# Where the first constants, logarithms and chunk-end powers are issued in a gated-attention and feed-forward kernel

## The chip, the cores and the metric

The kernel runs on one core of a Trainium2 chip. A core has a matrix engine (TensorE, PE in the profile), three engines for elementwise work (VectorE or DVE, ScalarE or ACT, GpSimd or POOL), and a fifth, SyncE or SP, that only issues DMA transfers. ScalarE and GpSimd can issue DMAs too, each on a queue of its own. Every engine takes its instructions in order and waits for others by semaphores. The metric is the device time of the whole kernel in microseconds (us); less is better.

## The reference

```python
# q, k, v, a_re, a_im: (4, 8, 768, 48): batch, heads, steps, head size
mag = sqrt(a_re**2 + a_im**2)
scale = minimum(mag, 0.999) / (mag + 1e-6)
a = (a_re + 1j * a_im) * scale
for t in range(768):
    S = a[t][:, None] * S + outer(k[t], v[t])     # complex 48 x 48 state per head
    y[t] = q[t] @ S.real
x = y as (3072 tokens, 384)
h = x @ w_in                                      # 384 x 2048
out = (h * cos(h)) @ w_out                        # 2048 x 384
```

The inputs of the attention part are float32; the two weight matrices arrive as float64.

## The kernel before, in words

The 768 steps of a batch are cut into 6 chunks of 128, the 128 steps on the partitions; two chunks make a group, so that 4 batches give 12 groups (G = 2). For a group, with a row of 384 numbers (8 heads of 48) for each step and chunk:

1. Logarithms (`log_steps`): ScalarE squares re and im, VectorE adds them, ScalarE takes a logarithm and exponentials, and some steps on VectorE refine the magnitude's logarithm (tile `lg`) and the tangent of half the angle (`tan`). Each `yield` ends a step, so that the order of the steps can be written out by hand.
2. Powers (`p_powers`, `even_steps`): a matmul with a triangular constant (`sums`, held in `upto`) adds the logarithms up over the steps (PSUM tile `lgs`), two exponentials make P and its inverse Q, and VectorE evens them out. P takes over the buffer of `lg`. The last row of P, the power at the chunk's end, is written to a DRAM scratch (`row`) and read back turned onto 2 x 48 partitions (`end`). Then `p_end` scales it.
3. Phases (`g_angle`, `g_phase`, `g_trig`): arctan, a matmul with the triangular constant divided by pi (`turns`, and `last` to carry the chunk before on), a wrap through an integer, then sine and cosine. Arctan and sine need another ScalarE table than logarithm and exponential.
4. Keys and queries (`p_apply`, `g_stack`, `f_turn`): products with P, Q, sine and cosine give `ks` and `qs`. In groups 0 and 1 TensorE transposes them with `ident`, and ScalarE copies them out of PSUM as kT and qT.
5. Scores, masked by `causal` (`sc`, `atm`), the state (`sp`, `state`, made with `end`), the chunk's rows (`yr`, in group 0), turned into `xT`, and then the two feed-forward products with the gate between (`hp`, `gate`, `op`; from group 2 on the second product is done in seven half-size products, `sum` and `op`).

For group 0 the two chunks are handled one by one (`one` and `two` are their logarithm steps); later groups go as wholes. In the first stage and up to group 1 the order on TensorE, ScalarE, VectorE and GpSimd is written out by hand: `chain` puts each instruction behind the last one of its engine. After that `weave` lays the steps of neighbouring groups into one order by shares of a group's time written beside each. `busy(n)` issues n matmuls on a constant tile whose result nobody reads.

The kernel's first DMAs: SyncE loads re and im of chunk 0, then of chunk 1, then k and q of both, then v (line 568); meanwhile ScalarE issues six constants (line 536), before anything else on its queue. GpSimd waits by a one-element copy (`wait_for`, line 1269) for im of chunk 1 and then issues the first four weight pieces (line 619), 768 KB each, as 64-bit words in one of four buffers; ScalarE (`lows`) and VectorE (`piece`) turn a piece into float32, and the next one is fetched when its buffer is free. Rows and ends go out over SyncE's queue (lines 828 and 831), for group 0 chunk by chunk, in among the loads of group 1. The DMAs on SyncE's and ScalarE's queues share eight completion semaphores by turns: a DMA waits, before it is issued, until the earlier DMA with the same semaphore has landed.

A check on the inputs (`verdict`) runs beside the work; `general_path`, the kernel for inputs that it doesn't hold for, is built behind a branch that isn't taken here.

Of the kernel before, what the change touches and what calls it, by code (L numbers as in the profile page):

```python
# [18 lines left out]
AF = mybir.ActivationFunctionType  # L19
ALU = mybir.AluOpType  # L20
# [467 lines left out]
def fast_path(ctx, tc, q, k, v, a_re, a_im, moe_w_in, moe_w_out, out, least, odd, wide,  # L488
# [7 lines left out]
    nc = tc.nc  # L496
    B, H, S, D = q.shape
    DM, DF = moe_w_in.shape
    C = 128
    NCH = S // C  # L500
    G = 2
# [10 lines left out]
    consts = ctx.enter_context(tc.tile_pool(name="consts", bufs=1))  # L512
# [8 lines left out]
    stage = {"pool": room.enter_context(tc.tile_pool(name="stage", bufs=1)), "bufs": 4}  # L521
# [4 lines left out]
    causal_np = (step_np[:, None] <= step_np[None, :]).astype(np.float32)  # L526


    sums_np = causal_np, np.roll(causal_np, -1, axis=0)
    last_np = np.zeros((C, C), np.float32)  # L530
    last_np[C - 1] = 1.0
    carry_np = np.where(step_np == C - 1, np.float32(math.pi), np.float32(0.0))[:, None]

    def constant(array, name, queue=nc.scalar, pool=consts):
        t = pool.tile(list(array.shape), F32, name=name)
        queue.dma_start(out=t, in_=nc.inline_tensor(array, name=name + "_const").ap())
        return t

    def scalar_tile(value, name):
        t = consts.tile([C, 1], F32, name=name)  # L540
        nc.vector.memset(t, value)
        return t

    X = [dict() for _ in range(NG)]
# [27 lines left out]
    for names in ("re", "im"), ("k", "q"), "v":  # L572
        for i in range(G):
            load(0, names, i)
    ident = constant(np.eye(C, dtype=np.float32), "ident", pool=stage["pool"])
    upto = [constant(sums_np[0], "sums", pool=stage["pool"])]
    turns = [constant(sums_np[0] * np.float32(1.0 / math.pi), "turns", pool=stage["pool"])]
    last = constant(last_np, "last", pool=stage["pool"])
    carry = constant(carry_np, "carry")
    causal = constant(causal_np * np.float32(0.25), "causal")  # L580
    tiny_b = scalar_tile(TINY, "tiny_b")
    one_b = scalar_tile(1.0, "one_b")
    half_pi_b = scalar_tile(math.pi / 2.0, "half_pi_b")
# [5 lines left out]
    RAW = stage["bufs"]  # L589
# [7 lines left out]
    def weight(dst, src):  # L597
        if src.dtype == F32:
            nc.sync.dma_start(out=dst, in_=src)
            return iter(()), lambda: None  # L600
        return from_double(dst, src)

    def from_double(dst, src):

        raw = fetched(src)
        lo = raw[0]
        return as_floats(dst, raw), lambda: scalar.activation(
            out=lo, in_=lo, func=AF.Identity, scale=2.0 ** -29, bias=carrier_b)
# [33 lines left out]
    out_scale = 2.0 if moe_w_out.dtype != F32 else 1.0  # L648

    late = {}
    tail = {}

    def chain(ins, engine="scalar"):

        if engine in tail:
            behind(ins, tail[engine])
        tail[engine] = ins

    def behind(ins, other):
        tc.add_manual_dep(ins.ins, other.ins.name, mybir.DependencyInfo(
            mybir.DependencyClass.NoSync, mybir.DependencyReason.DATA))

    def in_turn(**kw):

# [20 lines left out]
    vector, scalar = Ordered(nc.vector, "vector"), Ordered(nc.scalar, "scalar")  # L687
# [4 lines left out]
    def busy(count):  # L692

        ps = pa.tile([C, 512], F32, tag="a", name="busy")
        for _ in range(count):
            matmul(ps, lhsT=idle[:, 0:C].bitcast(F32R), rhs=idle.bitcast(F32R),
                   start=True, stop=True)
# [24 lines left out]
    def cut(t, i, n):  # L722
        return (flat(t) if len(t.shape) == 4 else t)[:, ds(i * DM, n * DM)]
# [11 lines left out]
    def log_steps(g, i, n):  # L735


        x = X[g]
        re, im = cut(x["re"], i, n), cut(x["im"], i, n)
        if i == 0:  # L740
            if g == 0:
                x["sin"] = temp("tan", 2)
            for name in "lg", "tan", "rs", "mag":
                x[name] = temp(name, 2 if name == "tan" else 1)
        m2, sq, rs, mag = (cut(x[name], i, n) for name in ("lg", "tan", "rs", "mag"))
        chain(nc.scalar.activation(out=m2, in_=re, func=AF.Square))
        chain(nc.scalar.activation(out=sq, in_=im, func=AF.Square))
        vector.tensor_tensor(out=m2, in0=m2, in1=sq, op=ALU.add)
        yield
        special(out=m2, in_=m2, func=AF.Ln, bias=tiny_b)  # L750
        special(out=mag, in_=m2, func=AF.Exp, scale=0.5)
        if g == 1:
            yield
        special(out=rs, in_=m2, func=AF.Exp, scale=-0.5)
        yield
        vector.scalar_tensor_tensor(out=mag, in0=re, scalar=0.0, in1=mag,
                                    op0=ALU.max, op1=ALU.add)
        vector.tensor_scalar(out=m2, in0=m2, scalar1=0.5, scalar2=math.log(CAP),
                             op0=ALU.mult, op1=ALU.min)
        yield  # L760
        special(out=rs, in_=rs, func=AF.Ln, scale=EPS, bias=one_b)
        special(out=sq, in_=mag, func=AF.Ln)
        special(out=sq, in_=sq, func=AF.Exp, scale=-1.0)
        yield
        vector.tensor_tensor(out=m2, in0=m2, in1=rs, op=ALU.subtract)
        yield

        lower = upper_half(g, m2, 1.0) if g >= PEG else None
        vector.tensor_tensor(out=mag, in0=mag, in1=sq, op=ALU.mult)
        if lower:  # L770
            lower()
        yield
        vector.scalar_tensor_tensor(out=sq, in0=mag, scalar=2.0, in1=sq,
                                    op0=ALU.subtract, op1=ALU.mult)
        yield
        vector.scalar_tensor_tensor(out=sq, in0=sq, scalar=-1.0, in1=im,
                                    op0=ALU.mult, op1=ALU.mult)
        yield
        junk = stage["pool"].tile([C, DM], BF16, tag="below", name="below", bufs=1) if n == 1 else re
        scalar.activation(out=junk, in_=re, func=AF.Relu, scale=-1.0,  # L780
                          accum_out=odd[:, ds(next(odds), 1)])
# [28 lines left out]
    def even_steps(g, i, n):  # L810


        x = X[g]
        u = cut(x["mag"], i, n)
        P, Q = cut(x["P"], i, n), cut(x["Q"], i, n)
        ins = [vector.scalar_tensor_tensor(out=u, in0=Q, scalar=HUGE, in1=P,
                                           op0=ALU.min, op1=ALU.mult)]
        yield
        for t in P, Q:
            ins.append(vector.scalar_tensor_tensor(out=t, in0=u, scalar=3.0, in1=t,  # L820
                                                   op0=ALU.subtract, op1=ALU.mult))
            yield

        for one_, what in zip(ins, ("carried", "split")):
            if what in x and g > PEG:
                behind(one_, x[what])
        row = x["row"][ds(i * DM, n * DM)]
        nc.sync.dma_start(out=row, in_=P[C - 1:C].rearrange("o x -> (o x)"))
        end = x["end"][:, ds(i * H, n * H)]
        for a in range(2):  # L830
            nc.sync.dma_start(out=end[ds(a * D, D)], in_=row.rearrange("(x d) -> d x", d=D))

    def p_even(g, i, n):
        for _ in even_steps(g, i, n):
# [50 lines left out]
    def g_trig(g, i, n):  # L885
        x = X[g]
        if i == 0:
            x["cos"] = temp("rs")
            if g:
                x["sin"] = temp("lo")  # L890
        cs, sn = cut(x["cos"], i, n), cut(x["sin"], i, n)
        ph = cut(x["tan"], i, n)
        vector.tensor_scalar(out=cs.bitcast(U32), in0=ph.bitcast(U32),
                                scalar1=0x7FFFFFFF, scalar2=None, op0=ALU.bitwise_and)
        special(out=sn, in_=ph, func=AF.Sin, scale=TWO_PI)
        special(out=cs, in_=cs, func=AF.Sin, scale=-TWO_PI, bias=half_pi_b)
# [370 lines left out]
    def wait_for(tile):  # L1267

        chain(nc.gpsimd.tensor_copy(out=after, in_=tile), "gpsimd")
# [10 lines left out]
    per = -(-len(guards) // (NG - 4))  # L1280
    load(1, ("v",))
    after = consts.tile([1, 1], F32, name="after")
    wait_for(X[0]["im"][0:1, G - 1, 0, 0:1])
    load(1, ("re", "im", "k", "q"))
    ones = constant(sums_np[1], "sums_turned", nc.sync, stage["pool"])
    exact = consts.tile([C, C], F32R, name="exact")
    alls = consts.tile([C, C], F32R, name="alls")
    chain(nc.gpsimd.tensor_copy(out=alls, in_=one_b.to_broadcast([C, C])), "gpsimd")
    parts = into + back
    pieces = [weight(dst, src) for dst, src in parts[:RAW]]  # L1290
    chain(nc.gpsimd.tensor_copy(out=exact, in_=ones), "gpsimd")
    Ordered.by_hand = "vector", "scalar"
    preload("natural_log_exp_and_others")
    busy(33)
    one, two = (log_steps(0, i, 1) for i in range(2))
    for _ in range(5):
        next(one), next(two)
    for i in range(2):
        p_powers(0, i)
    busy(10)  # L1300
    for _ in range(3):
        next(one), next(two)
    g_angle(0, 0, 2)
    next(one, None)
    for i in range(2):
        p_even(0, i, 1)
    g_phase(0, 0)
    next(two, None)
    g_trig(0, 0, 1)
    p_apply(0, 0, 1)  # L1310
    g_phase(0, 1)
    g_trig(0, 1, 1)
    busy(10)
    g_stack(0, 0, 1)
    p_apply(0, 1, 1)
# [340 lines left out]
```

## Time and profile before

| | |
|---|---|
| median of 3 runs | 660.46 us (659.95, 660.46, 667.34) |
| the profiled execution, its own time | 667.46 us |
| its span, first to last instruction | 665.7 us |
| TensorE busy | 650.7 us (98%), 4077 matmuls |
| VectorE busy | 490.6 us (74%) |
| ScalarE busy | 393.5 us (59%) |
| GpSimd busy | 27.9 us (4%) |
| DMA, mean | 143 GB/s, 94.90 MB |
| mean granted TensorE clock | 0.988 |

In a timeline a line gives the start in us, the duration, the engine (ACTq, SPq and POOLq are DMA issues on an engine's queue), the line of the kernel, the operation, the tiles and, in brackets, how long the engine had stood idle before and what released it. The chain is the work that ended last, followed back from the end. In a table of stages each row has the stretch, its length, the busy time of PE, PEld (weight loads), DVE, ACT and POOL with their instructions, and after these the granted TensorE clock as a share of full speed, the DMA engines' share and GB/s. Line 690 is the helper through which all matmuls go, line 679 that of VectorE's and many of ScalarE's instructions, so these are told apart by their tiles.

### The profile page before, as it was taken

How to read it: one execution, taken by the hardware profiler on the slowest of the kernel's cores; microseconds unless marked ns; L12 is line 12 of the kernel's file. 1: busy time of each engine (PE TensorE's matmuls, PEld its weight loads, DVE VectorE, ACT ScalarE, POOL GpSimd, SP SyncE). 2: the span in 40 equal slices, each digit the busy share in tenths (PEclk: the TensorE clock that was granted, in tenths of full speed). 3: DMA queues.
4: the chain of work that ended last, by engine and by line, in shares of the span. 5: the costliest groups of instructions: out<-in, count | busy, mean ns of one | idle time of the engine just before them, and what ended most of it. 6: DMA issues, size and time to landing. Idle time of an engine off the chain costs nothing.

```text
span 665.7 us, 10771 instructions
## 1 busy us (share of the span) xinstructions
PE 650.7 (98%) x4077; PEld 582.8 (88%) x4077; DVE 490.6 (74%) x797; ACT 393.5 (59%) x728; POOL 27.9 (4%) x47
## 2 busy tenths in 40 slices
PE   8899999999999999999999999999999999999996
PEld 6797977776899899899899899999999989999896
DVE  4977989869886887876877867876877868862251
ACT  6848696475484485485485485476476476432230
POOL 2011010000000010000000000000000000000000
PEclk9969999999999999999999999999999999999999
DMA  9946684727816827836837746846846853363001
GB/s 242 209 153 149 169 289 77 187 68 148 208 28 130 220 81 159 202 106 152 217 100 162 201 109 135 225 115 132 227 118 132 225 120 96 119 142 96 25 1 31
DMA packets 233626, 94.90 MB, mean 143 GB/s; under 512 B 208846, under 2 KB 222033, under 8 KB 233564
## 3 DMA queue, kind: packets, MB, share of 16 engines
q1 hardware_dynamic: 226924, 68.52, 45.1%
q0 software_dynamic: 5632, 25.17, 11.3%
q8 instruction: 34, 0.56, 0.4%
q10 hardware_dynamic: 1008, 0.43, 0.3%
q14 instruction: 28, 0.23, 0.1%
HBM read 69.28 MB, written 24.81 MB: 141 GB/s over the span
## 4 chain that ended last, share of the span: by engine, by line
PE 79%; DMA 7%; DVE 6%; ACT 2%; SPq 2%; issue 2%; POOL 0%; DVEq 0%; POOLq 0%
PE hp L690 31%; PE op L690 17%; PE sum L690 13%; PE sc L690 5%; PE yp L690 5%; PE sp L690 3%; PE phs L690 2%; DMA qT<-moved 2%; SPq L925 2%; PE lgs L690 1%; DMA raw<-in_moe_w_out_dram 1%; DMA xT<-x 1%; DVE mag L679 1%; PE yr L690 1%; DVE qs L679 1%
## 5 line engine op out<-in xcount | busy, mean ns | idle before, releaser
L690 PE MATMUL hp<-xT,w_in 128*128 128x256 f32 (+1 forms) x1176 | 255.3, 378 | 0.9 <-DMA xT<-x 0.9
L690 PEld LDWEIGHTS hp<-xT,w_in 128*128 128x128 f32 x1176 | 222.2, 193 | 31.9 <-DMA xT<-x 1.4
L710 ACT ACTIVATE gate<-hp,half_pi_b 128x512 f32<-128x512 f32 x96 | 66.0, 687 | 119.5 <-PE hp L690 119.5
L679 DVE TENSOR_TENSOR gate<-hp,gate 128x512 f32<-128x512 f32 x96 | 65.5, 682 | 48.2 <-ACT junk L679 48.1
L690 PE MATMUL op<-w_out,gate 128*128 128x192 f32 (+1 forms) x448 | 100.7, 374 | 0.0
L690 PEld LDWEIGHTS op<-w_out,gate 128*128 128x128 f32 x448 | 75.9, 190 | 16.9 <-issue 2.0
L679 ACT ACTIVATE junk<-hp 128x512 bf16<-128x512 f32 x96 | 56.7, 591 | 0.0
L679 DVE TENSOR_TENSOR atm<-sc,causal 128x512 f32<-128x512 f32 x48 | 32.8, 687 | 31.9 <-PE sc L690 31.9
L690 PE MATMUL sum<-t_s,s 128*128 128x192 f32 x320 | 55.4, 326 | 0.0
L690 PEld LDWEIGHTS sum<-t_s,s 128*128 128x128 f32 x320 | 52.5, 190 | 0.3 <-DVE ot L679 0.3
L679 ACT ACTIVATE ot<-sum 128x192 f32<-128x192 f32 x30 | 9.5, 320 | 70.4 <-PE sum L690 70.4
L690 PEld LDWEIGHTS sc<-qT,kT 96*128 96x128 f32 x384 | 47.5, 192 | 3.4 <-issue 1.2
L690 PE MATMUL sc<-qT,kT 96*128 96x128 f32 x384 | 49.3, 276 | 0.7 <-DMA qT<-moved 0.3
L679 DVE SCALAR_TENSOR_TENSOR ot<-op,ot 128x192 f32<-128x192 f32 x31 | 11.0, 355 | 33.8 <-ACT ot L679 24.8
L690 PE MATMUL yp<-atm,v 128*48 128x128 f32 x352 | 33.6, 277 | 1.1 <-DVE atm L679 1.1
L706 ACT ACT_TABLE_LOAD x24 | 30.8, 1283 | 4.0 <-DMA ident<-ident_const 3.6
L690 PEld LDWEIGHTS sp<-v,ks 128*96 128x96 f32 x320 | 29.7, 165 | 0.0
L690 PE MATMUL sp<-v,ks 128*96 128x48 f32 x320 | 29.7, 245 | 0.0
L690 PE MATMUL yp<-qT,state 96*48 96x128 f32 x304 | 29.6, 272 | 0.0
L690 PE MATMUL sum<-w_out,gate 128*128 128x192 f32 x160 | 29.6, 329 | 0.0
L690 PE MATMUL op<-t_a,gate 128*128 128x192 f32 x160 | 29.0, 332 | 0.0
L679 ACT COPY yT<-yp 48x512 f32<-48x512 f32 x44 | 25.3, 574 | 4.7 <-PE yp L690 4.3
(138 smaller groups left out, 981.9 us busy)
## 6 DMA issues: line engine op xcount, KB each, us to landing
moved<-tr SPq DMA_DIRECT2D x20, 768.0 KB
raw<-in_moe_w_in_dram POOLq DMA_DIRECT2D x16, 768.0 KB, 5.2
raw<-in_moe_w_out_dram POOLq DMA_DIRECT2D x16, 768.0 KB, 4.8
kT<-moved SPq DMA_DIRECT2D x40, 192.0 KB
qT<-moved SPq DMA_DIRECT2D x10, 768.0 KB
k<-in_k_dram SPq DMA_DIRECT2D x24, 192.0 KB
q<-in_q_dram SPq DMA_DIRECT2D x24, 192.0 KB
v<-in_v_dram SPq DMA_DIRECT2D x24, 192.0 KB
```

Source lines behind the costliest of these rows:

```text
L679: ins = getattr(self.engine, op)(**kw)
L690: chain(nc.tensor.matmul(out, **kw), "tensor")
L706: chain(nc.scalar.preload_act_table_set(table))
L710: chain(nc.scalar.activation(func=func, **kw))
L925: nc.sync.dma_start(out=X[g][name][:, ds(i * H, n * H), q4], in_=moved[q4])
```

## The change

It has four parts. (1) The constants `ident`, `sums`, `turns`, `last`, `causal` and `carry` are no longer issued by ScalarE at the start but by GpSimd: the first four behind the copy that waits for a load, `causal` after two weight pieces, `carry` after four. That copy now waits for re of chunk 1, not im. ScalarE's first instruction is then the load of its table. (2) The logarithm steps of chunk 0 go ahead of those of chunk 1, in an order written out; chunk 1's two squares are VectorE multiplies, with a `yield` between them. (3) The busy matmuls are dealt out anew: 25 before the powers rather than 33, six between the powers of the two chunks, ten after. (4) In group 0 the row of chunk-end powers is written once for both chunks and read back by two DMAs, all three on ScalarE's queue: the write before chunk 0's sine, the reads after chunk 1's cosine. Later groups keep SyncE's queue. As built, SyncE's first eight loads wait for no earlier DMA; nothing else moves on any engine, save that SyncE issues re and im of group 1 ahead of `sums_turned`.

```diff
-    def constant(array, name, queue=nc.scalar, pool=consts):
+    def constant(array, name, queue=None, pool=consts):
         t = pool.tile(list(array.shape), F32, name=name)
-        queue.dma_start(out=t, in_=nc.inline_tensor(array, name=name + "_const").ap())
+        put = (queue or nc.gpsimd).dma_start(
+            out=t, in_=nc.inline_tensor(array, name=name + "_const").ap())
+        if queue is None:
+            chain(put, "gpsimd")
         return t
...
-    ident = constant(np.eye(C, dtype=np.float32), "ident", pool=stage["pool"])
-    upto = [constant(sums_np[0], "sums", pool=stage["pool"])]
-    turns = [constant(sums_np[0] * np.float32(1.0 / math.pi), "turns", pool=stage["pool"])]
-    last = constant(last_np, "last", pool=stage["pool"])
-    carry = constant(carry_np, "carry")
-    causal = constant(causal_np * np.float32(0.25), "causal")
...
-        chain(nc.scalar.activation(out=m2, in_=re, func=AF.Square))
-        chain(nc.scalar.activation(out=sq, in_=im, func=AF.Square))
+        for out_, in_ in (m2, re), (sq, im):
+            if g == 0 and i > 0:
+                if in_ is im:
+                    yield
+                vector.tensor_tensor(out=out_, in0=in_, in1=in_, op=ALU.mult)
+            else:
+                chain(nc.scalar.activation(out=out_, in_=in_, func=AF.Square))
...
-        row = x["row"][ds(i * DM, n * DM)]
-        nc.sync.dma_start(out=row, in_=P[C - 1:C].rearrange("o x -> (o x)"))
-        end = x["end"][:, ds(i * H, n * H)]
+        if g > 0:
+            row_out(g, i, n, nc.sync)
+            row_back(g, i, n, nc.sync)
+
+    def row_out(g, i, n, queue):
+        P = cut(X[g]["P"], i, n)
+        queue.dma_start(out=X[g]["row"][ds(i * DM, n * DM)],
+                        in_=P[C - 1:C].rearrange("o x -> (o x)"))
+
+    def row_back(g, i, n, queue):
+        row = X[g]["row"][ds(i * DM, n * DM)]
+        end = X[g]["end"][:, ds(i * H, n * H)]
         for a in range(2):
-            nc.sync.dma_start(out=end[ds(a * D, D)], in_=row.rearrange("(x d) -> d x", d=D))
+            queue.dma_start(out=end[ds(a * D, D)], in_=row.rearrange("(x d) -> d x", d=D))
...
-    wait_for(X[0]["im"][0:1, G - 1, 0, 0:1])
+    wait_for(X[0]["re"][0:1, G - 1, 0, 0:1])
+    upto = [constant(sums_np[0], "sums", pool=stage["pool"])]
+    turns = [constant(sums_np[0] * np.float32(1.0 / math.pi), "turns", pool=stage["pool"])]
+    last = constant(last_np, "last", pool=stage["pool"])
+    ident = constant(np.eye(C, dtype=np.float32), "ident", pool=stage["pool"])
...
-    pieces = [weight(dst, src) for dst, src in parts[:RAW]]
+    pieces = [weight(dst, src) for dst, src in parts[:2]]
+    causal = constant(causal_np * np.float32(0.25), "causal")
+    pieces += [weight(dst, src) for dst, src in parts[2:RAW]]
+    carry = constant(carry_np, "carry")
...
-    busy(33)
+    busy(25)
     one, two = (log_steps(0, i, 1) for i in range(2))
-    for _ in range(5):
-        next(one), next(two)
+    for steps in one, two, one, one, two, one, one, two, one, two, two, one, two, one:
+        next(steps)
     for i in range(2):
         p_powers(0, i)
-    busy(10)
+        busy(6 + 4 * i)
     for _ in range(3):
-        next(one), next(two)
+        next(two)
     g_angle(0, 0, 2)
...
+    row_out(0, 0, G, scalar)
     g_trig(0, 0, 1)
     p_apply(0, 0, 1)
     g_phase(0, 1)
     g_trig(0, 1, 1)
+    row_back(0, 0, G, scalar)
     busy(10)
```

The helpers `chain` and `behind` only move up in the file, so that `constant` can use them.

More of the change, by code (lines that the diff above doesn't have):

```diff
@@ L532, in fast_path, with chain, behind @@
     carry_np = np.where(step_np == C - 1, np.float32(math.pi), np.float32(0.0))[:, None]
-    def constant(array, name, queue=nc.scalar, pool=consts):
+    late = {}
+    tail = {}
+    def chain(ins, engine="scalar"):
+        if engine in tail:
+            behind(ins, tail[engine])
+        tail[engine] = ins
+    def behind(ins, other):
+        tc.add_manual_dep(ins.ins, other.ins.name, mybir.DependencyInfo(
+            mybir.DependencyClass.NoSync, mybir.DependencyReason.DATA))
+    def constant(array, name, queue=None, pool=consts):
         t = pool.tile(list(array.shape), F32, name=name)
-        queue.dma_start(out=t, in_=nc.inline_tensor(array, name=name + "_const").ap())
+        put = (queue or nc.gpsimd).dma_start(
+            out=t, in_=nc.inline_tensor(array, name=name + "_const").ap())
+        if queue is None:
+            chain(put, "gpsimd")
         return t
@@ L648, in fast_path @@
     out_scale = 2.0 if moe_w_out.dtype != F32 else 1.0
[L652 to L663, printed above, removed]
     def in_turn(**kw):
```

## The prediction

> **What bounds the kernel now.** I read the page's engine shares first (TensorE is busy for 98% of 665.7 us, VectorE for 74%, ScalarE for 59%), then the timelines of the first 75 us, where every edited instruction lies, then the chain of work and the stages. From the timelines of ScalarE, VectorE and TensorE:
>
> ```profile
> 0.74 0.40 ACTq L536 DMA_DIRECT2D ident<-ident_const  x1
> ...
> 3.11 0.44 ACTq L536 DMA_DIRECT2D causal<-causal_const  x1
> 3.58 1.28 ACT L706 ACT_TABLE_LOAD   x1 [3.58 <-DMA ident<-ident_const]
> 4.88 0.52 ACT L746 ACTIVATE lg<-re 128x384 f32<-128x384 f32 x1
> ...
> 6.68 0.52 ACT L746 ACTIVATE lg<-re 128x384 f32<-128x384 f32 x1 [0.87 <-DMA re<-in_a_re_dram]
> 7.67 0.53 ACT L747 ACTIVATE tan<-im 128x384 f32<-128x384 f32 x1 [0.46 <-DMA im<-in_a_im_dram]
> ```
>
> Each line is start, duration, engine. ScalarE spends its first 3.6 us issuing constants, then 1.28 us on a table; it squares both chunks before it takes a logarithm, so chunk 0's logarithm waits for chunk 1's last load (7.67).
>
> ```profile
> 34.97 0.46 ACT L679 COPY rows<-yr 128x384 f32<-128x384 f32 x1
> ...
> 36.84 0.17 DVE L679 TENSOR_SCALAR end<-end 96x16 f32<-96x16 f32 x1 [2.69 <-DMA end<-row]
> ...
> 37.74 0.42 PE L690 MATMUL yr<-state,qT 96*128 96x48 f32 x2 [1.29 <-DVE state L679]
> ```
>
> VectorE stands 2.69 us for the row of powers read back through DRAM; TensorE then stands 1.29 us for the state made from it. The chain, with the DMA queue's part in it:
>
> ```profile
> 30.15 1.95 SPq L831
> 32.15 4.67 DMA end<-row
> 36.82 0.02 issue
> 36.84 0.18 DVE end L679
> ```
>
> The read-back was issued last on SyncE's queue, behind the second group's k and q. Last, the stages (length, granted clock after POOL's busy time):
>
> ```profile
> 34.85:38.26 3.41, 2.12 (x23) 2.00 (x22) 1.39 (x4) 2.63 (x5) 0.00 (x0) 1.00 0.30 94
> 38.26:51.92 13.66, 13.66 (x59) 12.69 (x58) 9.58 (x14) 5.24 (x8) 1.87 (x2) 0.50 0.59 160
> ```
>
> Right after that gap TensorE runs 13.66 us at half its clock though never idle: up to 6.83 us lost. The profiled execution took 667.46 us (span 665.7 plus 1.8 around it); the runs are 667.34, 660.46 and 659.95. Their 6.9 us is this price, so I read the median, 660.46, as a run without the half-clock stretch.
>
> **What the Trainium skill says.** "TensorE: Matmul & The Clock Gate", What's actually happening: the clock is set from activity in free-running windows of 3413 ns. The trace agrees in length (13.66 is four of them), not in recovery: the page lets one busy window restore the clock, here four passed. "ScalarE: Activation LUTs", What ACT_TABLE_LOAD costs: about 1283 ns plus a drain of 1380; the trace shows 1283 and no drain (the load at 15.64 begins 0.02 after the activation before it). "DMA: Bandwidth & Descriptors", Anatomy of one DMA: a GpSimd-issued transfer takes about 2.0 us plus bytes/436e3 per us; the trace has only 768 KB ones, median 5.2 and 4.8 us, above the formula's 3.8. The same page, Queues, rings and completion order: SyncE and ScalarE have separate rings which each DMA engine takes in turn. No run here shows that alone.
>
> **The change, part by part.**
>
> *Constants off ScalarE's queue, table first.* The six issues end at 3.55; the table can load at 0.74 to 2.02. ScalarE then waits for data: re of chunk 0 landed by 3.70 (its landing releases SyncE's fourth issue at 3.72). The first square moves from 4.88 to about 3.5. The constants' queue also held 3.4% of 16 engines' first 40 us, 1.36 us ahead of the last im, and made that im wait for a shared completion semaphore. So im of chunk 1 lands between 6.2 and 7.7 (as now). I take 6.3, keeping both ends.
>
> *The same constants on GpSimd.* They start once re of chunk 1 has landed (5.3 to 6.7). Small GpSimd issues aren't in the trace; the 768 KB ones cost 3.15/4 = 0.79 us each, an upper bound; I take 0.7. With the page's 2.15 us (an estimate), sums lands near 9 and its first user, lgs, cannot start before 25 busy matmuls at 10.60/33 = 0.32 each from 1.46, hence 9.5. Zero on the path; cover gone, up to 1 us. Turns (used near 16), last (18), ident (22) and causal (26) have 5 us or more. Weight DMAs behind four issues start 1 to 2 us later than 8.06; the first is read at 26.2 and landed about 8 us after issue, so nothing waits. Carry is for later groups.
>
> *Logs of chunk 0 ahead; chunk 1's squares on VectorE.* Two squares (0.52 each) leave ScalarE, two multiplies (0.56) join VectorE, which idles 4.32 and 1.82 us there. With rows' own durations: im square ends 4.5, sum 5.1, logarithm and two exponentials to 6.6, VectorE's two steps to 7.1, three activations to 8.1; chunk 1's im square and sum on VectorE 7.1 to 8.2; its logarithm 8.25, its last exponential 11.2 (before 14.1). Queued behind VectorE's waits for re and im of chunk 1 are chunk 0's steps; with today's landings all this is 1.3 later. lgs of chunk 1 stands behind six busy matmuls, about 12.0; its exponentials end 13.8, table 13.9 to 15.2 (before 15.64 to 16.92), arctan to 16.05. Gain 1.7 (1.3 with late loads). VectorE's even steps, which filled 16.5 to 19.6, are done by 16.2, so they don't take the place of that wait.
>
> *Row and ends on ScalarE.* One row issue before the sine and two end issues after chunk 1's cosine, about 0.3 + 2 x 0.46 (0.92 for the pair at 60.48) = 1.2 us of ScalarE. The row issue delays the sine by about 0.3; the ends run 21.5 to 22.4, and chunk 0's transposes deliver at about 22.5, so the copies of kT queued behind are hardly delayed. They wait for the row (issued 18.1; 2.75 us in today's case, so 20.9) and for the last two v loads, whose completion semaphores they reuse. Those are issued until 21.21 today; with earlier loads and later weights I put them near 16. The head's net shift at the first scores (25.90) is 1.7 - 0.2 = 1.5 us, range 0.3 to 2.
>
> The ends land near 26 rather than 36.8, so VectorE's 2.69 us goes, and TensorE's 1.29 with it: the second chunk's last atm (33.55 to 34.1 today) ends at 32.6 and end, least and state take 0.9 from there (36.84 to 37.69), 33.5, and TensorE asks for it at 36.36 - 1.5 = 34.9. Next late is nothing: SyncE has fewer issues ahead of the second group's loads.
>
> *Sum.* TensorE at that point is 1.5 + 1.29 = 2.8 us earlier. In a run at full clock VectorE is then the tighter one: from 36.84 to the second group's ks it idles only 5.31 + 0.62 us, less than the 6.83 TensorE would save. VectorE is earlier by 1.5 + 2.69 = 4.2, less about 0.8 where it now waits for ScalarE: it reaches the product of mag (41.15) at 36.95, and ScalarE's two logarithms and exponential before it end at 36.71 - 1.5 + 0.94 + 0.84 + 0.84, some 37.8. That leaves 3.4. I take 3.3, range 1.5 to 4.5. Against the profiled execution: 667.46 - 6.9 - 3.3 = 657.3; against the median, 660.46 - 3.3 = 657.2. All later work is ordered relative to this, with TensorE near 98%, so it carries to the end.
>
> **The rivals.**
> *A: the half clock stays or moves (slower).* Fewer busy matmuls (31 for 33) and a wait near 15.3 to 16.1 for the arctan and 17.7 to 18.2 for the first phase leave a window of 3.41 us about 62% busy, the share of the window that preceded the half clock (2.12 of 3.41); windows with 2.60 and 2.61 passed. It decides if the free-running window covers both gaps. Half clock from 18.6 to 32.3 halves about 10 us of dense work: 5.1 us, 662.4. If instead the small matmuls after 34, not the gap, caused it, 6.8: 664.0. For it: two of four executions had it. Against: the 1.29 us gap, the only one after 30, is gone.
> *B: ScalarE is blocked by the ends.* If v lands near 22.8 as today, or the row late, kT copies start at 23.8 rather than 22.5: 1.3 lost, 658.6. For: two waits on a queue with copies behind it. Against: v should be early.
> *C: sums late from GpSimd and loads no earlier.* Gain at the head 0.3, end gap still removed: 1.3 + 0.3, about 658.9. For: GpSimd's small issues are unmeasured.
> *D: a DMA or VectorE order downstream gives it all back:* 660.5. Against: the sequences after 40 us are the same.
>
> **How the numbers follow.** Forecast 657.2 (655.8 to 658.2) 0.55; A 0.18; B 0.12; C 0.10; D 0.05. The range runs from 655.5 to 663.0, with A's first form inside and its second left out. Two per cent is 13 us, about what a measurement of this kernel can tell from no change; no case reaches it (all gains together are under 5, the half clock twice would be 14), so within 2% gets 0.96, and 0.02 lies on either side.
>
> **What would show it.** Right: ScalarE's table at 0.7 and first square before 4; chunk 0's logarithm near 5; arctan near 15.2; the ends' issues before 22.5 with no idle time; no idle time of VectorE before end and of TensorE before yr's state, which starts near 35; clock 1.00 throughout. Wrong: lgs idle for sums, the kT copy released by a DMA, the clock at 0.50 anywhere, or the lead gone by the second group's scores (72.6).

## The result, and the profile after

| | before | after |
|---|---|---|
| median, 22 runs each | 661.07 us (657.56 to 669.00) | 660.05 us (657.33 to 666.48) |
| profiled execution, its own time | 667.46 us | 666.48 us |
| its span | 665.7 us | 664.6 us |
| mean granted TensorE clock in it | 0.988 | 0.992 |
| TensorE / VectorE / ScalarE busy | 650.7 / 490.6 / 393.5 us | 647.0 / 492.0 / 393.2 us |

The ratio after to before is 0.9978 with an interval of 0.9955 to 1.0000, which just reaches no change. The gain is 1.0 us, not the 3.3 forecast. The same two kernels, run again later (e9), gave 661.54 (30 runs) and 660.20 (22 runs): a gain of 1.3, ratio 0.9977 [0.9952, 1.0002]. Every ratio here leaves out runs more than 1.5% above the fastest of their kernel; the medians keep them. The runs over 664 us became rare: 8 of 22 before and 1 of 22 after, and 13 of 30 and 2 of 22 the second time.

I read the timelines in the order of the prediction's steps, the head of ScalarE first (columns as before: start, duration, engine, line, operation, idle time before and its releaser):

```profile
0.74 1.28 ACT L703 ACT_TABLE_LOAD   x1 [0.74 <-PEq L1660]
3.56 0.52 ACT L749 ACTIVATE lg<-re 128x384 f32<-128x384 f32 x1 [1.54 <-DMA re<-in_a_re_dram]
...
15.22 0.84 ACT L707 ACTIVATE tan<-tan 128x768 f32<-128x768 f32 x1
...
17.24 0.49 ACTq L676 DMA_DIRECT2D row<-lg  x1
...
22.69 1.17 ACTq L676 DMA_DIRECT2D end<-row  x2
23.90 1.07 ACT L676 COPY kT<-tp 96x512 f32<-96x512 f32 x2 [2.62 <-PE tp L948]
```

The same places before:

```profile
16.93 0.84 ACT L710 ACTIVATE tan<-tan 128x768 f32<-128x768 f32 x1
...
24.23 1.07 ACT L679 COPY kT<-tp 96x512 f32<-96x512 f32 x2 [1.00 <-PE tp L937]
...
25.90 2.05 PE L690 MATMUL sc<-qT,kT 96*128 96x128 f32 x16 [0.24 <-ACT qT L679]
```

The table loads at 0.74, the first square runs at 3.56 (before 4.88), the arctan at 15.22 (before 16.93): the 1.7 us at the head are there. Then ScalarE stands from 21.28, the end of its last sine or cosine, until the first `end` issue at 22.69, and the copies of kT come behind both issues, at 23.90. What the second of the two issues waited for stands in the chain of waits of the first 72 us:

```profile
11.08 12.44 DMA v<-in_v_dram
23.52 0.02 issue
23.55 0.31 ACTq L676
23.86 0.04 issue
23.90 1.07 ACT kT L676 x2
```

The last load of v began its issue at 11.08, ended it at 17.61 and landed at 23.52. The second `end` issue reuses its completion semaphore, so it ended 0.3 us after that landing, and kT followed. The first issue reuses the semaphore of the load before; by the landings kept in the trace that one came in at 22.67, and the row, which both issues need, at 22.10. (The timeline puts kT's idle time down to TensorE's transposes; the chain shows the DMA that really came last.) TensorE, in the same stretch:

```profile
22.53 1.08 PE L948 MATMUL tp<-ident,qs 128*96 128x128 f32 x8
25.50 3.73 PE L687 MATMUL sc<-qT,kT 96*128 96x128 f32 x16 [1.89 <-ACT qT L676]
```

The scores start at 25.50, only 0.4 before the old 25.90, and take 3.73 us, because the clock is at half. The stages (length, busy time of PE, PEld, DVE, ACT and POOL, granted clock, DMA share, GB/s):

```profile
15.35:18.76 3.41, 2.13 (x7) 1.12 (x7) 2.98 (x7) 2.80 (x8) 0.00 (x0) 1.00 1.05 366
22.17:25.59 3.42, 1.53 (x14) 1.17 (x12) 3.42 (x8) 1.69 (x4) 0.00 (x0) 1.00 1.13 178
25.59:32.41 6.82, 6.82 (x32) 6.65 (x33) 4.00 (x7) 3.84 (x6) 0.29 (x1) 0.50 0.95 156
```

The old stretch of half clock from 38.26 to 51.92 is gone; in this execution a shorter one follows the new gap, and another 3.4 us long comes at 93.85, behind a window (90.44 to 93.85) in which TensorE was busy for 1.45 us. At the place of the old gap VectorE now scales `end` at 36.80 without a wait.

### The profile page after: what moved, and what is told of

It reads as the page before. It is cut to its first block, busy times and chain, and to the rows that moved or that the text cites. A ratio compares the mean times of both kernels' runs of the same rounds, so it can differ in the third digit from the quotient of the medians.

```text
span 664.6 us, 10759 instructions
## 1 busy us (share of the span) xinstructions
PE 647.0 (97%) x4075; PEld 580.4 (87%) x4075; DVE 492.0 (74%) x799; ACT 393.2 (59%) x726; POOL 31.2 (5%) x53
## 3 DMA queue, kind: packets, MB, share of 16 engines
q0 software_dynamic: 5824, 25.50, 11.7%
## 4 chain that ended last, share of the span: by engine, by line
PE 81%; DMA 8%; ACT 4%; DVE 2%; SPq 2%; issue 1%; ACTq 0%; DVEq 0%
PE hp L687 33%; PE op L687 15%; PE sum L687 14%; PE sc L687 6%; PE yp L687 5%; PE sp L687 4%; PE phs L687 2%; DMA qT<-moved 2%; DMA v<-in_v_dram 2%; SPq L584 1%; DMA x<-yT 1%; DMA raw<-in_moe_w_out_dram 1%; PE lgs L687 1%; PE tp L948 1%; SPq L936 1%
## 5 line engine op out<-in xcount | busy, mean ns | idle before, releaser
L687 PEld LDWEIGHTS sc<-qT,kT 96*128 96x128 f32 x384 | 49.1, 197 | 5.2 <-ACT qT L676 2.1
L687 PE MATMUL sc<-qT,kT 96*128 96x128 f32 x384 | 50.9, 282 | 2.9 <-ACT qT L676 1.9
```

The lines of the kernel that those rows point to most:

```text
L687: chain(nc.tensor.matmul(out, **kw), "tensor")
```

## The experiments

All are variants of one of the two kernels; none leaves computation out. `busy` matmuls are fillers: nobody reads what they give. The kernels e1 to e4 ran on one chip, e5 to e8 on a second and e9 to e11 on a third, each beside runs of the kernel before on that chip. The last two columns split off the granted clock: runs with a mean clock under 0.996, and the median of those with 0.998 or more.

| kernel | median us (lowest to highest) | ratio to before [95%] | clock under 0.996 | median at 0.998 or more (runs) |
|---|---|---|---|---|
| before, chip 1 | 661.96 (658.27 to 673.60) | | 20 of 74 | 660.59 (38) |
| e1 rows and ends on SyncE | 664.34 (659.93 to 671.51) | 1.0029 [1.0003, 1.0055] | 17 of 22 | none |
| e2 rows and ends alone | 661.55 (659.68 to 665.27) | 0.9986 [0.9964, 1.0009] | 3 of 22 | 661.13 (13) |
| e3 rows and ends on GpSimd | 658.25 (656.10 to 665.26) | 0.9948 [0.9922, 0.9973] | 2 of 21 | 658.21 (17) |
| e4 v behind the ends | 658.79 (656.08 to 663.09) | 0.9945 [0.9923, 0.9967] | 0 of 22 | 658.68 (19) |
| before, chip 2 | 664.55 (659.88 to 672.16) | | 13 of 27 | 662.36 (9) |
| e5 after, gap filled | 658.89 (658.51 to 659.57) | 0.9885 [0.9841, 0.9929] | 0 of 6 | 658.89 (6) |
| e6 before, gap filled | 663.62 (661.37 to 667.98) | 0.9986 [0.9965, 1.0007] | 2 of 22 | 663.11 (15) |
| e7 weights later | 658.87 (658.06 to 659.79) | 0.9884 [0.9840, 0.9928] | 0 of 6 | 658.83 (5) |
| e8 e3 with the old logarithms | 658.85 (657.12 to 659.52) | 0.9881 [0.9836, 0.9926] | 0 of 6 | 658.85 (6) |
| before, chip 3 | 661.54 (657.47 to 668.74) | | 12 of 30 | 660.19 (15) |
| e9 after, again | 660.20 (657.53 to 664.88) | 0.9977 [0.9952, 1.0002] | 5 of 22 | 659.78 (14) |
| e10 after, gap filled (as e5) | 658.36 (657.17 to 660.28) | 0.9914 [0.9872, 0.9957] | 0 of 7 | 658.36 (7) |
| e11 ends on GpSimd (as e3) | 657.78 (656.34 to 662.53) | 0.9908 [0.9866, 0.9950] | 1 of 8 | 657.24 (6) |

The kernel before differs by 3 us from chip to chip, so each row is to be compared with its own chip. For the kernels with 6 to 8 runs the ratio gives more than the medians (e11: 6.1 us and 3.8); it seems to go by the first runs of the kernel before, which were longer than its later ones (the first 8 on chip 3 have the median 665.47, the other 22 have 660.89). The gains in the text are differences of medians. "At full clock" means the last column.

**e1: the fourth part undone.** Rows and ends of group 0 go back to SyncE's queue, chunk by chunk.

```diff
-        if g > 0:
-            row_out(g, i, n, nc.sync)
-            row_back(g, i, n, nc.sync)
+        row_out(g, i, n, nc.sync)
+        row_back(g, i, n, nc.sync)
...
-    row_out(0, 0, G, scalar)
...
-    row_back(0, 0, G, scalar)
```

> The changed kernel with the fourth part undone: rows and ends of group 0 again per chunk on SyncE's queue. Theory (the head's lead of some 1.6 us is real and is given back because ScalarE stands before the ends' issues): with no DMA on ScalarE the first kT copy comes near 22.3 (23.90 in the changed kernel, 24.23 before), the first scores near 24.0; but the ends land near 36 again, VectorE waits for them by 3 us or more and TensorE by 2.5 us or more before yr's state; the median is 660 to 661, with the runs near 667 back. Rival (the head's lead counts by itself, the ends never mattered): 659.0 or less. Second rival (the head never gained): scores at 25.5 or later.

Measured: kT at 22.09 and scores at 23.70, so without the `end` issues on ScalarE nothing blocks there. But the old wait returns, larger. From the list of waits of e1:

```profile
DVE end L676 <- DMA end<-row: 4.7, 1, 4.7
PE yr L687 <- DVE state L676: 3.4, 1, 3.4
```

And its stages:

```profile
34.59:38.00 3.41, 0.36 (x3) 0.36 (x4) 1.23 (x4) 0.85 (x2) 0.00 (x0) 1.00 0.23 19
38.00:51.65 13.65, 13.65 (x60) 12.74 (x60) 9.74 (x14) 4.93 (x8) 1.88 (x2) 0.50 0.58 158
```

TensorE was busy 0.36 of the 3.41 us ahead of the half clock. The head's whole lead turned into idle time before `end`, and the low clock, which came in 20 of 74 runs before, came in 17 of 22. So parts 1 to 3 alone make the kernel slower, by 1.9 us [0.2, 3.6] (the ratio times 661.96). The wait was foreseen; that it would make half clock the rule, and the median 664.34 instead of 660 to 661, was not.

**e2: the fourth part alone,** on the kernel before.

```diff
+        if g > 0:
+            row_out(g, i, n, nc.sync)
+            row_back(g, i, n, nc.sync)
...
+    row_out(0, 0, G, scalar)
     g_trig(0, 0, 1)
...
     g_trig(0, 1, 1)
+    row_back(0, 0, G, scalar)
```

> The kernel before with the fourth part alone: row and ends of group 0 over ScalarE's queue. Theory: TensorE's wait of 1.29 us for the state goes and ScalarE stands less than 1 us before the ends, since the head is as late as before and the v loads whose semaphores they reuse land near 23.5: median 659.0 to 660.5, and the runs near 667 become rare. Rival (the gain of the changed kernel comes from the head): 661 as before, with the runs near 667 as frequent.

Measured: the ends are issued at 22.84 for 0.97 us and kT starts at 24.08 behind its transposes, not behind a load: with the old, later head the ends find hardly anything to wait for. The gap before the state is gone. The total is 661.55, a gain of 0.4 that its interval does not tell from none, and short of the 659.0 to 660.5 expected; at full clock it isn't faster at all (661.13 against 660.59). The low clock came less often (3 of 22 runs against 20 of 74), but these are too few to be a finding.

**e3 (and e11, the same kernel on another chip): row and ends on GpSimd's queue,** behind its constants and weights, so that ScalarE issues nothing in the stage.

```diff
-        queue.dma_start(out=X[g]["row"][ds(i * DM, n * DM)],
-                        in_=P[C - 1:C].rearrange("o x -> (o x)"))
+        queue.dma_start(out=X[g]["row"][ds(i * DM, n * DM)].unsqueeze(0), in_=P[C - 1:C])
...
-    chain(nc.gpsimd.tensor_copy(out=exact, in_=ones), "gpsimd")
-    Ordered.by_hand = "vector", "scalar"
+    Ordered.by_hand = "vector", "scalar", "gpsimd"
...
-    row_out(0, 0, G, scalar)
+    row_out(0, 0, G, pool)
...
-    row_back(0, 0, G, scalar)
+    row_back(0, 0, G, pool)
+    chain(nc.gpsimd.tensor_copy(out=exact, in_=ones), "gpsimd")
```

The row's write also has another form here and in e8, for all groups: it goes out in 16 pieces of 192 bytes, not as one of 3072. That is not what gained, for the row landed at 22.25 in e3 and at 21.92 in e11, beside 22.10 in the changed kernel, and e4 and e7 gain without it.

> The changed kernel with row and ends of group 0 on GpSimd's queue, behind carry, where nothing else is due until 31. Theory: ScalarE no longer stands before the kT copies, kT starts near 22.3 and the scores near 24.0, the ends land before 33, TensorE has no gap above 0.6 us between 22 and 36 and no half clock there: median 657.0 to 658.8. Rival (a lead in the first 40 us is absorbed later, and only the end gap counts): 659.5 to 660.5, as the changed kernel.

> The kernel with the ends on GpSimd once more, beside the changed kernel. Theory: median 1.5 to 3 us below the changed kernel and 3 to 5 below the kernel before. Rival: within 0.7 of the changed kernel.

GpSimd's timeline in e3, ScalarE's copy and TensorE's scores after it:

```profile
16.93 0.53 POOL L676 DMA_DIRECT2D row<-lg  x1 [4.42 <-DVE lg L676]
22.54 1.52 POOL L676 DMA_DIRECT2D end<-row  x2 [5.08 <-DMA row<-lg]
```

```profile
22.16 1.07 ACT L676 COPY kT<-tp 96x512 f32<-96x512 f32 x2 [1.00 <-PE tp L948]
```

```profile
23.77 2.05 PE L688 MATMUL sc<-qT,kT 96*128 96x128 f32 x16 [0.27 <-ACT qT L676]
```

The wait is now on an engine that has nothing due; v landed as late as ever (23.11 in e3). kT waits for its transposes alone and starts 1.74 us earlier than in the changed kernel (22.16 against 23.90), the scores 1.73 earlier. VectorE still gets `end` in time: in e11 it scales it at 31.91 with no idle time. The gain over before is 3.7 us (e3) and 3.8 (e11). Among the runs at full clock, for which the forecast of 3.3 was made, it is 2.4 and 3.0; the rest is what the low-clock runs add to the median of before.

**e4: group 1's v loads issued behind the ends,** with the ends still on ScalarE. They then reuse the semaphores of group 0's v.

```diff
-    load(1, ("v",))
...
     row_back(0, 0, G, scalar)
+    load(1, ("v",), put=lambda **kw: behind(nc.sync.dma_start(**kw), tail["scalar"]))
```

> The changed kernel with group 1's v loads issued behind the ends, so that the ends reuse the semaphores of group 0's v, which land some 8 us earlier; the ends stay on ScalarE. Theory (ScalarE waits for the landing of v, not for the row): the ends issue at 21.3 to 21.6, the kT copy starts by 22.6, median 657.2 to 659.0. Rival (the row's own landing, 5 us after its issue, is what ScalarE waits for): the ends issue at 22.5 as before, kT near 23.8, median as the changed kernel, 659.5 to 660.5.

```profile
21.88 0.91 ACTq L676 DMA_DIRECT2D end<-row  x2
22.83 1.07 ACT L676 COPY kT<-tp 96x512 f32<-96x512 f32 x2 [1.64 <-PE tp L948]
```

The ends now depend on loads that landed long before, and kT comes 1.07 us earlier than in the changed kernel (the two v loads are also out of the traffic until 22.45, so it is not the dependence alone that was changed); the scores start at 24.44 after 0.91 us of idle time. What holds the ends now is the row: the chain of e4 has its write from 17.16 to 21.80 (4.64 us), where I had counted 2.75. The gain over before is 3.2 us, 1.9 at full clock.

**e7: the third and fourth weight pieces fetched later,** the ends as in the changed kernel.

```diff
-    pieces += [weight(dst, src) for dst, src in parts[2:RAW]]
     carry = constant(carry_np, "carry")
     chain(nc.gpsimd.tensor_copy(out=exact, in_=ones), "gpsimd")
+    pieces += [weight(dst, src) for dst, src in parts[2:RAW]]
```

> The changed kernel with the third and fourth weight pieces issued behind the copy that waits for sums_turned, some 15 us later; their readers come at 40. Theory (the four weight pieces, 3.1 MB, hold up group 1's v on the shared DMA engines, and ScalarE's ends wait for that v): v lands by 20, the ends issue at 21.3 to 21.8 with at most 0.5 us of standing, kT near 22.8, median 657.5 to 659.0. Rival (v is slow by itself, 192-byte pieces): the ends issue at 22.5 or later, median as the changed kernel; or the late pieces hold up VectorE near 40 and it is slower than 661.

ScalarE's timeline in e7:

```profile
20.48 0.91 ACTq L676 DMA_DIRECT2D end<-row  x2
22.06 1.07 ACT L676 COPY kT<-tp 96x512 f32<-96x512 f32 x2 [0.99 <-PE tp L948]
```

With 1.5 MB fewer in flight the issues are through by 21.4, before kT is due. By the landings kept in the traces the last v load came in at 19.20, where the changed kernel had it at 23.52 and, in the second profile, at 23.62; the row took 2.40 us from its issue to its landing instead of 4.86. So it is the weights that hold up v, and the row too. The account of the changed kernel's DMA over the first 40 us (packets, MB, share of 16 engines) shows how:

```profile
q1 hardware_dynamic: 20944, 4.00, 53.9%
q0 software_dynamic: 1232, 4.26, 30.7%
```

SyncE's queue moves 191 bytes a packet (4.00 MB by 20944), GpSimd's 3.5 KB. The Trainium skill, "DMA: Bandwidth & Descriptors", Queues, rings and completion order, says that each DMA engine goes round the queues packet by packet, and Issuing engines are not separate DMA queues in the same page that all share the same 16 engines. e7 agrees in kind: taking two pieces out of the one queue let the other's v through. That the packet-wise turn is the reason is not shown here.

**e8: e3 with the old order of the logarithms, squares and fillers,** so parts 1 and 4 without 2 and 3.

```diff
-        for out_, in_ in (m2, re), (sq, im):
...
+        chain(nc.scalar.activation(out=m2, in_=re, func=AF.Square))
+        chain(nc.scalar.activation(out=sq, in_=im, func=AF.Square))
...
-    for steps in one, two, one, one, two, one, one, two, one, two, two, one, two, one:
-        next(steps)
+    for _ in range(5):
+        next(one), next(two)
```

> The kernel before with the first part (constants on GpSimd, table first) and the ends on GpSimd, but the logarithms' order, ScalarE's squares and the busy matmuls as before. It sizes the first part of the head: theory: with the loads landing up to 1.5 us earlier the first logarithm starts near 6.7 (8.10 before, 5.94 in the changed kernel) and the arctan near 15.7 (16.93 before, 15.22 in the changed kernel), so the constants give some 1.2 of the head's 1.7 us; median 658.3 to 660, between the kernel before and the one with the ends on GpSimd (658.25). Rival (the order of the logarithms carries the head): arctan at 16.4 or later.

Measured: the arctan starts at 15.77, against 16.93 before and 15.22 after. Of the head's 1.7 us the constants' move gives 1.16 and the logarithms' order 0.55. At the first scores the order of the logarithms and the fillers are worth 0.9 (24.69 here, 23.77 in e3). In the total that is within the noise (658.85 beside e7's 658.87).

**e5 (and e10, the same kernel): the changed kernel with eight fillers in the new gap.**

```diff
     turn(0, 0)
+    busy(8)
     lows(0, 1)
```

> The changed kernel with eight busy matmuls (1.7 us at full clock) between chunk 0's transposes and its first scores, where TensorE stood 1.89 us. Theory (an idle stretch there, where it falls into a clock window, halves the clock of the scores behind it): no half clock between 20 and 45 us in the profile, the scores still near 25.5 because ScalarE's block stays; median 659 to 660, none above 664. Rival (the small matmuls of this stage halve the clock, not the gap): half clock still seen after 22 in the profile or as many runs at 661 to 663 as in the changed kernel (8 of 22 above 661.6).

> The kernel with eight busy matmuls ahead of the first scores once more, beside the changed kernel. Theory: no half clock before 45 us, median 0.5 to 2 us below the changed kernel, and about 2 above the one with the ends on GpSimd (the scores start near 25.8 rather than 23.8). Rival (the gap does not matter for the clock): median equal to the changed kernel within 0.4.

ScalarE in e10, then TensorE:

```profile
23.28 1.08 ACTq L676 DMA_DIRECT2D end<-row  x2
24.39 1.07 ACT L676 COPY kT<-tp 96x512 f32<-96x512 f32 x2 [2.98 <-DMA v<-in_v_dram]
```

```profile
23.51 2.09 PE L687 MATMUL busy<-idle 128*128 128x512 f32 x8
26.00 2.05 PE L687 MATMUL sc<-qT,kT 96*128 96x128 f32 x16 [0.40 <-ACT qT L676]
```

ScalarE is blocked as long as in the changed kernel and the scores come no earlier, yet the median is 658.36 (7 runs) beside 660.20 (22 runs) for e9 on the same chip, 1.8 us less, and no run of 13 has a clock under 0.996. That the cost of the block comes in part through the clock is likely but not shown: of the 1.8 us, 1.4 are there among the runs at full clock too (658.36 against 659.78), which I can't place, and 5 of 22 low runs against none of 13 are few. Beside e11 I expected e10 about 2 us above; it is 0.6 above, 1.1 at full clock.

**e9: the changed kernel once more,** with the second profile of it.

> The changed kernel as it is, on one chip with the next two, so that they can be compared with it. Theory: it loses some 2 us to ScalarE standing before the ends' issues and up to 3 more in the runs where the clock halves behind that gap; median 1.5 to 3 us above the kernel with the ends on GpSimd and 0.5 to 2 above the one with the gap filled, with a wider spread than both. Rival (the gains of those two were the chip's): all three within 0.7 us.

```profile
22.74 1.21 ACTq L676 DMA_DIRECT2D end<-row  x2
23.99 1.07 ACT L676 COPY kT<-tp 96x512 f32<-96x512 f32 x2 [2.95 <-DMA v<-in_v_dram]
```

```profile
25.59 2.05 PE L687 MATMUL sc<-qT,kT 96*128 96x128 f32 x16 [2.22 <-ACT qT L676]
```

The block is the same within 0.1 us, so it belongs to the kernel; the gap is 2.22 us, longer than in the first profile, and the scores take 2.05 us, at full clock. Why the clock stayed, the trace itself shows. All changes of the clock within an execution, in all 13 profiles, lie whole multiples of 3.413 us apart, so the edges of its windows can be counted on from any one change. In e9 the clock changes at 656.50, in the last moments; counted back, edges lie at 21.62 and 25.03, and the second cuts the gap (23.37 to 25.59) in two:

```profile
21.62:25.03 3.41, 1.75 (x16) 1.39 (x14) 3.41 (x9) 1.04 (x3) 0.00 (x0) 1.00 1.23 193
25.03:28.44 3.41, 2.85 (x25) 2.85 (x26) 1.94 (x5) 3.11 (x6) 0.05 (x1) 1.00 1.35 194
```

In the first profile the whole gap of 1.89 us fell into one window, 22.17 to 25.59, which left 1.53 us busy.

**e6: the kernel before with six fillers in its old gap.**

```diff
     f_columns(0)
+    busy(6)
     f_rows(1, 0, HH)
```

> The kernel before with six busy matmuls (1.3 us) ahead of the second chunk's rows, where TensorE stood 1.29 us for the state. Theory (that gap is what halves the clock in the runs near 667): the start of yr's state stays near 37.7, no half clock after it, and the runs above 664, a third of those of the kernel before, are gone; median 660 to 661. Rival (the clock is halved by the small matmuls before the gap): a third of the runs still above 664.

Measured: 663.62, against an expectation of 660 to 661 that had an earlier chip's level in it; the kernel before stands at 664.55 on this one. The gain of 0.9 is not told from none. The profile has no half clock in its first 100 us, and 2 of 22 runs have a clock under 0.996, against 13 of 27. Still 9 of 22 runs are above 664 (15 of 27 before), the rival's sign, though on a chip whose level is this high it says little. At full clock it is 0.75 slower than before (663.11 against 662.36, nine runs), so the fillers may cost what they save. That the gap before the state brought the low clock is supported; the price of it per run stays rough.

**Where the lead is.** The start of the chunk sums (`sp`) on TensorE, read from the timelines, in us:

| | before | e6 | after | e9 | e3 | e11 |
|---|---|---|---|---|---|---|
| group 0, second chunk | 34.42 | 34.33 | 37.33 | 34.12 | 32.29 | 32.20 |
| group 1, first | 74.41 | 68.53 | 69.37 | 66.17 | 64.35 | 64.25 |
| end of the span | 665.6 | 663.8 | 664.6 | 658.3 | 655.9 | 655.8 |

Before and e6 part between the first two rows: the half clock of before costs 5.8 us. After and e9 part by 3.2 for the shorter one. With full clock in all, e9 is 1.8 to 1.9 us behind e3 and e11: this is the block. The kernel with the fourth part alone, e2, starts group 1 at 66.33, beside 66.17 for e9: with ScalarE blocked, parts 1 to 3 bring the second group next to nothing. Against e6 the leads at group 1 are 2.4 (e9) and 4.3 (e11); they are upper bounds, since e6 carries its fillers. From there to the end the profiles take between 591.2 (before) and 595.2 us (after, e6), a spread that goes with no part of the change. Each of `after` and e6 has one more half-clock window in it, worth up to 1.7 us; without one, e9, e3 and e11 take 591.6 to 592.2 and the blocked e10 590.2, so a difference of a microsecond or two between the ends of two profiles can't be read.

## Why the prediction was wrong

The forecast was 657.2, a gain of 3.3; the gain was 1.0, and 1.3 in the second comparison. The mechanism was right and one step in it failed.

**The step that failed** is in the costing of rows and ends on ScalarE: v's loads, "issued until 21.21 today; with earlier loads and later weights I put them near 16", and from it "the copies of kT queued behind are hardly delayed". The issues ended about there, at 17.61 (14.37 in e9), but the last load landed at 23.52 (23.62 in e9), no earlier than the 23.50 of the kernel before, because all four weight pieces were moving beside it (with two of them later, in e7, it landed at 19.20). I had taken the end of the issue as if it were near the landing, and I gave the row 2.75 us from issue to landing where the changed kernel, e3, e4, e9 and e11 show 4.6 to 5.3. So kT came at 23.90 instead of 22.5 and the head's net shift at the scores was 0.4 us instead of 1.5. That is rival B, word for word ("kT copies start at 23.8"), to which I gave 0.12. Two edits that leave ScalarE's instructions alone, e4 (other semaphores) and e7 (v and row earlier), bring kT back to 22.83 and 22.06. Moving the issues off ScalarE, e3, brings it to 22.16. Each of the three then gains 3.2 us or more over before, and 1.9 to 3.5 at full clock.

**The size of B** was also too small: 1.3 was written, 1.9 us is what e9 lacks beside e11 at the second group, and the gap of 1.89 to 2.22 us that the block leaves in TensorE can bring rival A's half clock, at a place that A didn't name. 3.3 less 1.9 is 1.4, near the 1.0 and 1.3 measured, but in part by luck: those medians include low-clock runs on both sides. At full clock the change gains 0.4 (659.78 against 660.19), and e3 and e11 gain 2.4 and 3.0, so the 3.3 was also somewhat too much, though within its range of 1.5 to 4.5.

**What held.** The table at 0.74, the first square at 3.56 (3.5 forecast), the arctan at 15.22 (15.2), so the 1.7 at the head, though chunk 0's logarithm came at 5.94 and not near 5; the split in it is 1.16 for the constants and 0.55 for the logarithms (e8). Sums from GpSimd: issued at 5.89 for 0.68 us (0.7 taken), lgs at 9.58 (9.5) with its last wait on `lg`, so rival C is out. That was close: sums landed at 9.45, 3.6 us after its issue and not the 2.15 estimated, and `lg` was ready at 9.50. The wait for `end` and TensorE's 1.29 us went, and nothing came late there. The second group's lead of 3.4 us that I worked out for VectorE's stage is found only when the block is gone: 4.3 at most in e11, less what e6's fillers hold. Rival D, that a later order gives all back, is refuted by e3 and e11, whose lead reaches the end.

**The clock.** I took 660.46 as a run without the half clock, and two of three chips agree: at a clock of 0.998 or more the kernel before has 660.59 and 660.19, on the other 662.36. Of the two forms of A neither came as written: the window of 15.35 to 18.76, 2.13 of 3.41 us busy, passed at full clock, as thin as the 2.12 that preceded the half clock before. The forecast "clock 1.00 throughout" was wrong in the first profile, right in the second but for its last moments. Lower clock is less frequent after than before on chip 3 (5 of 22 runs against 12 of 30), too few to be a finding; against e1 (17 of 22, on another chip) it is one. What decides in a given run can be read from the 13 profiles by counting windows as for e9. Between the start and the last microseconds there are six half-clock stretches, and each begins behind a window in which TensorE was busy for 0.36 (e1), 1.07 (e2, at 612.72), 1.45 and 1.53 (after), 1.56 (e6, at 615.07) or 2.12 us (before). Every other window, from 1.75 us up, passed. So in these profiles what counts is how much of a gap falls into one window, and where the windows lie differs from run to run. The window of 2.12, full of small matmuls, is the exception, and why it halved the clock where 2.02 (e7), 2.07 (e9) and 2.13 passed stays open. It was not tried to move the windows on purpose.

**The version that beats both** is e3: the change with its row and ends on GpSimd, 657.78 us (e11, 8 runs) beside 660.20 and 661.54 on one chip; six of the eight runs are below all but one of e9's 22.

## What to carry to other kernels

A DMA issued from a compute engine's queue is an instruction that can wait, for its source and for whatever earlier DMA has the same completion semaphore, and all the compute behind it waits too (here kT's copies, from 21.28 to 23.90): give it to an engine with nothing due (3.8 us gained in place of 1.3 here). When a prediction needs a load to have landed, find the landing and what else is on the DMA engines then, not the end of its issue. Removing one wait ahead of a step that is still late elsewhere only makes the second wait longer, and on TensorE a longer gap may also cost clock: the head alone (e1) was a loss, the read-back alone (e2) no measurable gain, and both together, unblocked, were worth 3.7 us, 2.4 of them at full clock.

## What the runs showed of the hardware that was not expected

- A half-clock stretch lasted one, two or four windows of 3.41 us (3.42 at 93.85, 6.82 at 25.59, 13.66 before), with TensorE busy throughout. The Trainium skill, "TensorE: Matmul & The Clock Gate", What's actually happening, lets one busy window restore the clock; only the shortest stretch agrees.
- A gap of 2.22 us (e9) left the clock alone, where one of 1.89 had halved it: an edge of the clock's windows cut the longer one in two (1.75 and 2.85 us busy of 3.41), the shorter one lay in one window (1.53). Windows of 2.12 and 2.13 us went one way and the other.
- Eight filler matmuls, 2.09 us in a gap, made the kernel 1.8 us faster and its runs closer together (657.17 to 660.28 in 7 runs beside 657.53 to 664.88 in 22).
- Writing a row of 3 KB to DRAM took 4.5 to 5.3 us from the start of its issue to its landing beside weight and v loads (2.4 in e7, with two weight pieces fewer), and a 192 KB load 12.4 us, of which its issue alone took 6.5.
- A 64 KB issue on GpSimd took 0.55 to 0.68 us, a 768 KB one 0.75, a row 0.53: the price of an issue hardly depends on its size.
